# First loads, the first gate and up products, and the output's stores rearranged in a fused SSM-convolution and gated-MLP kernel

## The chip, the cores and the metric

The kernel runs on one core of one Trainium2 chip. A core has a matrix engine (TensorE, PE in the profile), a vector engine (VectorE, DVE), a scalar engine (ScalarE, ACT), GpSimd (POOL) and SyncE (SP), which here only issues DMAs. Each engine takes its instructions in the order in which the program holds them. The metric is the device time of one execution in microseconds (us). Something within about 1% cannot be told from no change with this kernel's three runs.

## The reference

All tensors are bf16, S = 2048 tokens, D = 640 columns, F = 1728. From `x = A_q`, and its layer norm `xn`:

```python
xn  = layernorm(x)
kv  = (sum over t of shift(k, t) * shift_k[:, t]) * v      # 4 taps
y   = causal_conv(kv, ssm_k) + kv * ssm_D                  # long convolution, by FFT in the reference
out = x + xn * y + (sigmoid(xn @ w_gate) * (xn @ w_up)) @ w_down
```

## The kernel before, in words

**Layout.** Token 16p + b lies on partition p in block b, so x is a tile of 128 partitions, 16 blocks and 640 columns. Two strands of work share the engines.

**The MLP strand** goes by four groups t of 512 tokens (four blocks each). Layer norm of a block: statistics on DVE (`ln_stats`), the reciprocal root on POOL (`ln_rstd`), `ln_nmr` on DVE, and `xn` on ACT, DVE or POOL (`ln_xn`). `xn_tr` transposes a block of xn on PE (five 128x128 transposes into PSUM) and ACT or DVE copies it to `xnT`. Then for each of 13 slices fc of 128 columns of F: `gate(fc)` is five matmuls of 512 columns and a sigmoid on ACT; `up(fc)` is five matmuls and a product on DVE into `hT`. `both` does the remaining 64 columns of gate and up at once. `down` is 14 matmuls in two parts of seven for one block and one half of the output's columns, and an addition on DVE into x. These PSUM tiles rotate through the four buffers of pool `psG`.

**The convolution strand** goes by five chunks c of 128 columns. DVE makes kv (`kv_op`, 16 operations per chunk); `h_tr` transposes the filter (16 transposes on PE, two copies on ACT); `add_D` on POOL puts ssm_D into its first tap. The long convolution is a two-stage Fourier transform as matmuls: `st1` (8 per chunk, ACT evicts), `wr1` to DRAM, `rd2` back in another order, `st2` (4 per chunk, ACT evicts), products on DVE (`prod`), `inv1` (2 per chunk, ACT evicts), `wr2` to DRAM, `rdb` back, and `inv2` (2 per chunk, 16 matmuls each), after which DVE multiplies by xn (L409) and adds to x (L410). `rdb` has one buffer `bi`, so the second read of a chunk is issued only when the first `inv2` of that chunk is done. These PSUM tiles rotate through the two buffers of pool `psC`.

**Order.** All of it is written out by a planner at build time. The head (the loads, the layer norm and transposes of group 0, `h_tr(0)`) is written by hand. Then the planner walks PE's time with its own costs (`free`, `ready`, durations in each step), emits the MLP steps `seq` one after another, and puts convolution steps between them when its model says that their inputs are there. `side` issues DMAs, POOL steps and DVE steps; `DUE` says from which MLP step on the next group's layer norm goes ahead of kv on DVE, and `slack` how far ahead of time each kind of load may be issued. The planner runs nothing on the chip: what it fixes is the order of the instructions on each engine and on the DMA queue of SP. At most eight DMAs are outstanding, since the ninth waits for the semaphore of the first.

**The head before** (L413 to L437): ACT's queue issues the filter h of chunk 0 (512 KB); SP's queue issues x block by block (four DMAs of 160 KB), w columns 0 to 255 of gate and up, the taps, k and v of chunk 0, w columns 256 to 767, and the table S1. PE does the four blocks' transposes, then `h_tr(0, 0)` and `h_tr(0, 1)`, then `gate(0)`.

**The end before.** Each of the 16 blocks is stored by one DMA of 160 KB (`store`, L265), which needs the last chunk's `inv2` of its half (blocks 0 to 7 or 8 to 15) and both `down` additions of its block. All 16 stand behind every other DMA on SP's queue.

Of the kernel before, what the change touches and what calls it, by code (L numbers as in the profile page):

```python
# [19 lines left out]
P = 128  # L20
# [37 lines left out]
def kernel(  # L58
# [67 lines left out]
    def load_x(eng, g, n=4):  # L126
        for b in range(4 * g, 4 * g + 4, n):
            eng.dma_start(x[:, b:b + n, :], xr[:, b:b + n, :])
# [79 lines left out]
            eng.tensor_scalar(xn[:, b, :], x[:, b, :], d["rstd"][:, i:i + 1], d["nmr"][:, i:i + 1],  # L208
                              op0=ALU.mult, op1=ALU.add)

    def xn_tr(g, i, eng="act"):

        pt = psG.tile([P, NC, P], BF16, name="pt", tag="g")
        for c in range(NC):
            nc.tensor.transpose(pt[:, c, :], xn[:, 4 * g + i, c * P:(c + 1) * P], ident[:])  # L215
        dst = xnT[:, :, i * P:(i + 1) * P]
        if eng == "act":
            nc.scalar.copy(out=dst, in_=pt[:, :, :])
        else:
            nc.vector.tensor_copy(dst, pt[:, :, :])  # L220


    sig = {}

    def gate(fc):
        pg = psG.tile([P, 512], F32, name="pg", tag="g")
        for c in range(NC):
            nc.tensor.matmul(pg[:, :], lhsT=w[:, c, fc * P:(fc + 1) * P], rhs=xnT[:, c, :],  # L228
                             start=(c == 0), stop=(c == NC - 1))
        sig[fc] = cv.tile([P, 512], BF16, name="sig", bufs=2)  # L230
        nc.scalar.activation(sig[fc][:, :], pg[:, :], ACT.Sigmoid)  # L231

    def up(fc):
        pu = psG.tile([P, 512], F32, name="pu", tag="g")
        for c in range(NC):
            nc.tensor.matmul(pu[:, :], lhsT=w[:, c, UP + fc * P:UP + (fc + 1) * P], rhs=xnT[:, c, :],  # L236
                             start=(c == 0), stop=(c == NC - 1))
        nc.vector.tensor_tensor(hT[:, fc, :], sig[fc][:, :], pu[:, :], ALU.mult)  # L238

    def both():  # L240
# [20 lines left out]
        if part == 1:  # L261
            nc.vector.tensor_tensor(x[:, b, es], pd[:, :], x[:, b, es], ALU.add)  # L262

    def store(b):
        sync.dma_start(outr[:, b, :], x[:, b, :])  # L265


    def add_D(c):
# [141 lines left out]
        nc.vector.tensor_tensor(x[:, bs, cs], x[:, bs, cs], yx[:, :, :], ALU.add)  # L410


    load_h(0, nc.scalar, 0, 0, S)  # L413
    load_x(sync, 0, 1)
    load_w(sync, 0, 256)
    load_taps(0)
    load_halo(0)
    load_k(0, 0, NB)
    load_v(0, 0, NB)
    load_w(sync, 256, 768)  # L420
    sync.dma_start(S1t[:], S1d.ap())

    for i in range(4):
        ln_stats(0, i)
        ln_rstd(0, i, i + 1)
        if i:
            ln_nmr(0, i - 1, i)
            ln_xn(0, i - 1, "act")
        if i == 2:
            xn_tr(0, 0)  # L430
        if i == 3:
            xn_tr(0, 1)
    ln_nmr(0, 3, 4)
    ln_xn(0, 3)
    xn_tr(0, 2)
    xn_tr(0, 3, "dve")
    add_D(0)  # L437
    h_tr(0, 0)
    h_tr(0, 1)

    free = dict(PE=15.5, ACT=15.5, DVE=15.0, POOL=14.0, SP=15.0, DMA=20.0)
    ready = dict(S1=22.0, kx0=15.0, v0=17.0)
    ready.update({("w", f): 14.0 if f < 2 else 18.5 for f in range(6)})
    ready.update({("taps", 0): 15.0,
                  ("h", 0, 0): 16.0, ("h", 0, 1): 17.0})
    count = dict(C=0, G=0)  # L450
    BIG = 1e9

    def when(need):
# [6 lines left out]
    def emit(step):  # L460
        fn, args, ops = step
        ops = ops()
        fn(*args)
        for eng, dur, need, make in ops:
            at = when(need)
            if eng == "DMA":
                free["SP"] = max(free["SP"], at) + 0.45
                free["DMA"] = max(free["DMA"], free["SP"] + 1.4) + dur
                end = free["DMA"] + 0.7
            else:  # L470
                free[eng] = max(free[eng], at) + dur
# [93 lines left out]
    for c in range(NC):  # L565
        if c:
# [8 lines left out]
            for i in range(4):  # L575
# [3 lines left out]
            chains["pool2"] = chains.get("pool2", [])  # L579
            chains["pool2"].append((taps, (c,), lambda c=c: [("POOL", 0.75, [("sraw", c), ("kvn", c - 1, 13)],  # L580
                                                              [("taps", c)])]))
            chains["front"] += [s_htr(c, 0), s_htr(c, 1)]
        chains["kv"] += [s_kv(c, [8 * h + n for n in ns]) for h in range(2)
                         for ns in ((0,), (1, 2), (3, 4), (5, 6), (7,))]
        chains["front"] += [s_st1(c, n) for n in range(8)]
# [18 lines left out]

    bulk = chains["bulk"]
    bulk.append((sync.dma_start, (SMt[:], SMd.ap()), lambda: [("DMA", 0.2, [], ["SM"])]))
    bulk += [s_w(768, 1280), s_x(1), s_w(1280, FF)]
    bulk += chains["sp_k"][:5] + [s_wd(0, 7), s_wd(7, NFC)] + chains["sp_v"][:4] + chains["sp_h"][:2]
    del chains["sp_k"][:5], chains["sp_v"][:4], chains["sp_h"][:2]
    chains["bulk2"] = bulk = [s_x(2), s_x(3)]  # L610
    bulk.append((sync.dma_start, (TBt[:], TBd.ap()), lambda: [("DMA", 2.9, [], ["TB"])]))
# [54 lines left out]
    for b in range(NB):  # L666
        last = [("xa", NC - 1, b // 8), ("dn", b, 1)]
        chains["out"].append(s_load(store, (b,), 0.7, last, []))

    pos = {k: 0 for k in chains}  # L670

# [93 lines left out]
```

## Time and profile before

| what | us |
|---|---|
| median of 3 runs (252.27 to 253.85) | 253.43 |
| the profiled execution | 254.8 |
| its span, from the first to the last recorded event | 252.9 |
| PE busy, 2428 matmuls | 235.4 |
| DVE busy | 179.0 |
| ACT busy | 150.0 |
| POOL busy | 27.8 |
| first matmul starts | 8.28 |
| first `gate` starts | 13.72 |
| last matmul ends | 248.79 |

The span is cut into 40 slices of 6.3 us on the page, and a digit there is a busy share in tenths. The timeline gives an instruction or a run of equal ones by its start and length; a note in brackets says how long its engine had been idle and what ended it. A matmul's recorded length includes its way through the array (379 ns for 512 columns), while the distance between starts of equal matmuls is the pace (216 ns for 512 columns). The profiled execution is 1.4 us above the median of the runs; sums below are made against it and then moved to the median.

### The profile page before, as it was taken

The numbers are of one execution on the slowest core, as the hardware profiler recorded it, in microseconds if no ns is written. First come the engines' busy times: TensorE is split into PE (matmuls) and PEld (weight loads), VectorE is DVE, ScalarE is ACT, GpSimd is POOL, SyncE is SP. The second block draws the span as 40 slices with busy tenths as digits, with TensorE's granted clock in tenths as the row PEclk, the third lists the DMA queues.
The fourth block names the chain that finished last, engine by engine and source line by source line (L and its number), as shares of the span: only waits on it lengthen the run. The fifth ranks groups of instructions, "written<-read, shape, count | busy, mean of one in ns | idle before, by whom it ended". The sixth has DMA issues, their size and how long they took to land.

```text
span 252.9 us, 5862 instructions
## 1 busy us (share of the span) xinstructions
PE 235.4 (93%) x2428; PEld 138.3 (55%) x2428; DVE 179.0 (71%) x312; ACT 150.0 (59%) x186; POOL 27.8 (11%) x40
## 2 busy tenths in 40 slices
PE   0499999889999999999999999999999989999993
PEld 0454455557755554556765545656666435445772
DVE  2749999499889999599999992156718284674361
ACT  2744471428988788873676678966577754463000
POOL 4300118020001070701100000000000000000000
PEclk9999999999999999999999999999999999999999
DMA  6999989999998999879755423697247582303285
GB/s 183 264 326 345 351 183 358 294 259 234 268 264 310 246 307 289 218 209 345 237 184 176 132 95 135 233 281 271 83 161 216 131 238 91 86 3 84 84 287 212
DMA packets 84310, 54.84 MB, mean 217 GB/s; under 512 B 46844, under 2 KB 77372, under 8 KB 84028
## 3 DMA queue, kind: packets, MB, share of 16 engines
q1 hardware_dynamic: 83996, 53.95, 72.8%
q10 hardware_dynamic: 288, 0.52, 0.6%
q8 instruction: 19, 0.31, 0.5%
q14 instruction: 7, 0.06, 0.1%
HBM read 36.12 MB, written 18.35 MB: 215 GB/s over the span
## 4 chain that ended last, share of the span: by engine, by line
PE 69%; DMA 23%; DVE 2%; ACT 2%; SPq 1%; issue 1%; ACTq 0%
PE pg L228 17%; PE pu L236 17%; PE pd L259 17%; DMA bi<-d 9%; DMA d<-t 6%; PE ps L319 5%; PE psb L405 4%; DMA TBt<-tabTB 3%; PE psa L377 3%; PE ps L347 3%; DMA t<-d 2%; DMA x<-in_A_q_dram 2%; PE pht L277 2%; PE pt L215 2%; DMA d<-ao 2%; DVE st L187 1%
## 5 line engine op out<-in xcount | busy, mean ns | idle before, releaser
L259 PE MATMUL pd<-wd,hT 128*128 128x320 bf16 x448 | 65.5, 300 | 0.0
L228 PE MATMUL pg<-xnT,w 128*128 128x512 bf16 x260 | 64.8, 380 | 0.0
L236 PE MATMUL pu<-xnT,w 128*128 128x512 bf16 x260 | 64.7, 380 | 0.0
L238 DVE TENSOR_TENSOR hT<-sig,pu 128x512 bf16<-128x512 bf16 x52 | 35.3, 681 | 35.7 <-PE pu L236 25.8
L259 PEld LDWEIGHTS <-hT 128*128 128x128 bf16 x448 | 42.5, 98 | 17.7 <-issue 1.8
L231 ACT ACTIVATE sig<-pg 128x512 bf16<-128x512 f32 x52 | 31.2, 602 | 31.8 <-PE pg L228 31.4
L350 ACT CAST xz<-ps 128x1024 bf16<-128x1024 f32 x40 | 38.5, 1017 | 12.0 <-PE ps L347 11.7
L322 ACT CAST t<-ps 128x1024 bf16<-128x1024 f32 x40 | 39.1, 1018 | 9.6 <-PE ps L319 5.4
L228 PEld LDWEIGHTS <-w 128*128 128x128 bf16 x260 | 24.8, 98 | 27.2 <-issue 1.3
L236 PEld LDWEIGHTS <-w 128*128 128x128 bf16 x260 | 24.5, 98 | 27.2 <-issue 1.4
L262 DVE TENSOR_TENSOR x<-pd,x 128x320 bf16<-128x320 f32 x32 | 15.5, 488 | 14.8 <-PE pd L259 14.4
L361 DVE TENSOR_TENSOR xz<-xz 128x2048 bf16<-128x2048 bf16 x20 | 24.5, 1224 | 0.6
L382 ACT CAST ao<-psa 128x1024 bf16<-128x1024 f32 x20 | 19.3, 1017 | 8.1 <-PE psa L377 4.5
L298 DVE TENSOR_TENSOR acc<-acc,tmp 128x1024 bf16<-128x1024 bf16 x30 | 21.9, 729 | 1.0
L319 PE MATMUL ps<-kvh,S1t 128*128 128x256 bf16 x160 | 21.9, 273 | 0.0
L296 DVE TENSOR_TENSOR tmp<-kx,sc 128x1024 bf16<-128x1024 bf16 x30 | 20.6, 686 | 0.1
L319 PEld LDWEIGHTS <-S1t 128*128 128x128 bf16 x160 | 15.4, 98 | 5.8 <-issue 0.3
L187 DVE BATCH_NORM_STATS2 st<-x 128x6 f32<-128x320 bf16 x32 | 14.0, 478 | 4.6 <-DMA x<-in_A_q_dram 4.6
L409 DVE TENSOR_TENSOR yx<-psb,xn 128x1024 bf16<-128x1024 f32 x10 | 12.2, 1220 | 6.2 <-PE psb L405 6.1
L215 PE MATMUL pt<-ident,xn 128*128 128x128 bf16 x80 | 7.7, 242 | 9.5 <-ACT xn L204 9.5
L278 ACT COPY kvh<-pht 128x1024 bf16<-128x1024 bf16 x10 | 10.1, 1017 | 8.2 <-PE pht L277 8.1
L359 DVE STREAM_SHUFFLE xz<-xz 128x512 f32<-128x512 f32 x20 | 14.5, 725 | 0.0
(40 smaller groups left out, 149.1 us busy)
## 6 DMA issues: line engine op xcount, KB each, us to landing
d<-t SPq DMA_DIRECT2D x20, 512.0 KB, 4.1
t<-d SPq DMA_DIRECT2D x20, 512.0 KB, 5.7
d<-ao SPq DMA_DIRECT2D x10, 512.0 KB, 4.5
bi<-d SPq DMA_DIRECT2D x10, 512.0 KB, 4.4
out_dram<-x SPq DMA_DIRECT2D x16, 160.0 KB, 2.6
kx<-in_A_k_dram SPq DMA_DIRECT2D x16, 128.0 KB, 3.8
kvh<-in_A_v_dram SPq DMA_DIRECT2D x16, 128.0 KB, 4.4
hn<-in_A_ssm_k_dram SPq DMA_DIRECT2D x8, 256.0 KB, 4.2
```

The costliest lines, as they stand in the source:

```text
L228: nc.tensor.matmul(pg[:, :], lhsT=w[:, c, fc * P:(fc + 1) * P], rhs=xnT[:, c, :], start=(c == 0), stop=(c == NC - 1))
L231: nc.scalar.activation(sig[fc][:, :], pg[:, :], ACT.Sigmoid)
L236: nc.tensor.matmul(pu[:, :], lhsT=w[:, c, UP + fc * P:UP + (fc + 1) * P], rhs=xnT[:, c, :], start=(c == 0), stop=(c == NC - 1))
L238: nc.vector.tensor_tensor(hT[:, fc, :], sig[fc][:, :], pu[:, :], ALU.mult)
L259: nc.tensor.matmul(pd[:, :], lhsT=hT[:, fc, bb * P:(bb + 1) * P], rhs=wd[:, fc, es], start=(fc == 0), stop=(fc == NFC - 1))
L296: nc.vector.tensor_tensor(d["tmp"][:, :, :], kx[:, lo + 3 - m:hi + 3 - m, :], sb(m), ALU.mult)
L298: nc.vector.tensor_tensor(d["acc"][:, :, :], d["acc"][:, :, :], d["tmp"][:, :, :], ALU.add)
L319: nc.tensor.matmul(ps[:, i, :], lhsT=S1[:, b, h, :], rhs=cin[c]["kvh"][:, b, :, :], start=True, stop=True)
L322: nc.scalar.copy(out=d["t1"][:, o:o + 4, :, :].rearrange("p b s c -> p b (s c)"), in_=ps[:, :, :])
L350: nc.scalar.copy(out=d["xz"][:, 0:2, 4 * n:4 * n + 4, :].rearrange("p s k c -> p k s c"), in_=ps[n].rearrange("p q e s c -> p (q e) s c"))
L361: nc.vector.tensor_tensor(xz[:, 1:3, :, :], xz[:, 0:1, :, :].to_broadcast((P, 2, 8, P)), xz[:, 1:3, :, :], ALU.mult)
L382: nc.scalar.copy(out=dst[:, 2 * n:2 * n + 2, :, :], in_=ps[n].rearrange("p g (s f) -> p g s f", s=2))
```

## The change

- The four blocks of x go out alternately from SP's and ACT's queues, as the first DMAs of each; h of chunk 0 follows on ACT's queue. w is loaded in pieces of 256 columns, interleaved with the taps, k and v; S1 moves behind w columns 768 to 1023.
- `gate` and `up` of fc = 0 and 1 are done in halves of 256 tokens (`half`): the first halves, as soon as two blocks are transposed; then the second halves. The transposes of blocks 2 and 3 stand between the first halves and use `psC`. One of the copies moves from ACT to DVE.
- `h_tr(0, *)` leaves the hand-written head and is placed by the planner like the other chunks'; in the new order it stands right behind the halves.
- The planner's starting state, `DUE`, `slack` and the latency it allows a DMA (0.7 to 1.2) are changed, so the order of the whole program changes.
- `store` takes a range of blocks and columns: columns 0 to 511 of blocks 0 to 11 in pairs, as soon as chunk 3 and `down` are done; columns 512 to 639 of blocks 0 to 7 and of 8 to 11 in one DMA each; blocks 12 to 15 whole.

```diff
-    def xn_tr(g, i, eng="act"):
+    def xn_tr(g, i, eng="act", pool=None):
-        pt = psG.tile([P, NC, P], BF16, name="pt", tag="g")
+        if pool is None:
+            pt = psG.tile([P, NC, P], BF16, name="pt", tag="g")
+        else:
+            pt = pool.tile([P, NC, P], BF16, name="pt", tag="c")
...
+    halves = {}
+    def half(u, fc, n):
+        if n == 0:
+            halves[u, fc] = psG.tile([P, 512], F32, name="pg", tag="g")
+        ns = slice(256 * n, 256 * n + 256)
+        o = u * UP + fc * P
+        for c in range(NC):
+            nc.tensor.matmul(halves[u, fc][:, ns], lhsT=w[:, c, o:o + P], rhs=xnT[:, c, ns],
+                             start=(c == 0), stop=(c == NC - 1))
     def gate(fc):
+        if (0, fc) in halves:
+            half(0, fc, 1)
+            pg = halves.pop((0, fc))
+        else:
...
-    def store(b):
-        sync.dma_start(outr[:, b, :], x[:, b, :])
+    def store(b0, b1, lo, hi):
+        sync.dma_start(outr[:, b0:b1, lo:hi], x[:, b0:b1, lo:hi])
...
-    load_h(0, nc.scalar, 0, 0, S)
-    load_x(sync, 0, 1)
+    for i in range(4):
+        (sync, nc.scalar)[i % 2].dma_start(x[:, i, :], xr[:, i, :])
     load_w(sync, 0, 256)
     load_taps(0)
+    load_h(0, nc.scalar, 0, 0, S)
+    load_w(sync, 256, 512)
     load_halo(0)
     load_k(0, 0, NB)
+    load_w(sync, 512, 768)
     load_v(0, 0, NB)
-    load_w(sync, 256, 768)
-    sync.dma_start(S1t[:], S1d.ap())
...
-        if i == 2:
-            xn_tr(0, 0)
-        if i == 3:
-            xn_tr(0, 1)
+        if i > 1:
+            xn_tr(0, i - 2, ("act", "dve")[i - 2])
     ln_nmr(0, 3, 4)
     ln_xn(0, 3)
-    xn_tr(0, 2)
-    xn_tr(0, 3, "dve")
+    for fc in range(2):
+        half(0, fc, 0)
+        if fc == 0:
+            xn_tr(0, 2, pool=psC)
+        else:
+            xn_tr(0, 3, "dve", pool=psC)
+        half(1, fc, 0)
+    for fc in range(2):
+        gate(fc)
+        up(fc)
     add_D(0)
-    h_tr(0, 0)
-    h_tr(0, 1)
...
-                end = free["DMA"] + 0.7
+                end = free["DMA"] + 1.2
...
-            chains["front"] += [s_htr(c, 0), s_htr(c, 1)]
+        chains["front"] += [s_htr(c, 0), s_htr(c, 1)]
...
-    bulk += [s_w(768, 1280), s_x(1), s_w(1280, FF)]
-    bulk += chains["sp_k"][:5] + [s_wd(0, 7), s_wd(7, NFC)] + chains["sp_v"][:4] + chains["sp_h"][:2]
+    bulk.append(s_w(768, 1024))
+    bulk.append((sync.dma_start, (S1t[:], S1d.ap()), lambda: [("DMA", 2.9, [], ["S1"])]))
+    bulk += [s_w(1024, 1280), s_w(1280, FF), s_x(1), s_wd(0, 7), s_wd(7, NFC)]
+    bulk += chains["sp_k"][:5] + chains["sp_v"][:4] + chains["sp_h"][:2]
...
-        for fc in range(13):
+        for fc in range(0 if t else 2, 13):
...
+    for b in range(0, 12, 2):
+        chains["out"].append(s_load(store, (b, b + 2, 0, 4 * P), 1.2,
+                                    [("xa", NC - 2, b // 8), ("dn", b + 1, 1)], []))
+    for b in (0, 8):
+        e = 8 if b == 0 else 12
+        chains["out"].append(s_load(store, (b, e, 4 * P, DM), 0.25 * (e - b),
+                                    [("xa", NC - 1, b // 8), ("dn", e - 1, 1)], []))
+    for b in range(12, NB):
+        chains["out"].append(s_load(store, (b, b + 1, 0, DM), 0.7,
+                                    [("xa", NC - 1, 1), ("dn", b, 1)], []))
...
-    DUE = (14, 50, 58)
-    slack = dict(bulk=3.0, sp_k=1.5, sp_v=1.5, sp_h=1.5, bulk2=1.5)
+    DUE = (8, 48, 68)
+    slack = dict(bulk=3.0, sp_k=3.0, sp_v=3.0, sp_h=2.0, bulk2=2.0)
```

More of the change, by code (lines that the diff above doesn't have):

```diff
@@ L223 @@
     sig = {}
-    def gate(fc):
[L226 to L229, printed above, removed]
+    halves = {}
[7 more added lines that the diff above has]
+                             start=(c == 0), stop=(c == NC - 1))
+    def gate(fc):
+        if (0, fc) in halves:
+            half(0, fc, 1)
+            pg = halves.pop((0, fc))
+        else:
+            pg = psG.tile([P, 512], F32, name="pg", tag="g")
+            for c in range(NC):
+                nc.tensor.matmul(pg[:, :], lhsT=w[:, c, fc * P:(fc + 1) * P], rhs=xnT[:, c, :],
+                                 start=(c == 0), stop=(c == NC - 1))
         sig[fc] = cv.tile([P, 512], BF16, name="sig", bufs=2)
@@ L233, in up @@
     def up(fc):
[L234 to L237, printed above, removed]
+        if (1, fc) in halves:
+            half(1, fc, 1)
+            pu = halves.pop((1, fc))
+        else:
+            pu = psG.tile([P, 512], F32, name="pu", tag="g")
+            for c in range(NC):
+                nc.tensor.matmul(pu[:, :], lhsT=w[:, c, UP + fc * P:UP + (fc + 1) * P], rhs=xnT[:, c, :],
+                                 start=(c == 0), stop=(c == NC - 1))
         nc.vector.tensor_tensor(hT[:, fc, :], sig[fc][:, :], pu[:, :], ALU.mult)
@@ L428 @@
             ln_xn(0, i - 1, "act")
-        if i == 2:
-            xn_tr(0, 0)
-        if i == 3:
-            xn_tr(0, 1)
+        if i > 1:
+            xn_tr(0, i - 2, ("act", "dve")[i - 2])
     ln_nmr(0, 3, 4)
     ln_xn(0, 3)
-    xn_tr(0, 2)
-    xn_tr(0, 3, "dve")
-    add_D(0)
-    h_tr(0, 0)
-    h_tr(0, 1)
[L445 to L450, printed above, removed]
+    for fc in range(2):
+        half(0, fc, 0)
+        if fc == 0:
+            xn_tr(0, 2, pool=psC)
+        else:
+            xn_tr(0, 3, "dve", pool=psC)
[3 more added lines that the diff above has]
+        up(fc)
+    add_D(0)
+    free = dict(PE=14.5, ACT=14.7, DVE=15.2, POOL=11.0, SP=11.0, DMA=17.0)
+    ready = dict(kx0=15.0, v0=19.0)
+    ready.update({("w", f): 14.0 if f < 4 else 17.0 for f in range(6)})
+    ready.update({("taps", 0): 14.0, ("D", 0): 14.0, ("va", 0): 0.0})
+    ready.update({("C", 0): 11.0, ("C", 1): 12.0})
+    ready.update({("G", k): 13.0 + 0.6 * k for k in range(4)})
+    count = dict(C=2, G=4)
     BIG = 1e9
@@ L665 @@
     per = 27 + 16 + 4
-    for b in range(NB):
-        last = [("xa", NC - 1, b // 8), ("dn", b, 1)]
-        chains["out"].append(s_load(store, (b,), 0.7, last, []))
+    for b in range(0, 12, 2):
[8 more added lines that the diff above has]
+                                    [("xa", NC - 1, 1), ("dn", b, 1)], []))
     pos = {k: 0 for k in chains}
```

## The prediction

> **What bounds the kernel now.** I read the slices first, then the chain of work that ended last, the waits of PE, and the timeline at both ends.
>
> ```profile
> PE   0499999889999999999999999999999989999993
> DVE  2749999499889999599999992156718284674361
> DMA  6999989999998999879755423697247582303285
> ...
> PE 69%; DMA 23%; DVE 2%; ACT 2%; SPq 1%; issue 1%; ACTq 0%
> ```
>
> PE is full from slice 3 to slice 37 and carries 69% of the chain; the DMA share is reads and writes between the convolution's stages. DVE is nearly full up to slice 24, the DMA engines up to slice 19. So the time is PE's work, plus PE's late start, plus its waits, plus the tail behind its last product.
>
> To separate these I put PE's instructions in their order and added their paces from the timeline (start to start): 1.08 us for five matmuls of 512 columns, 0.95 for seven of `down`, 0.44 for an `st1`, 0.47 for `st2`, 0.88 for `inv1`, 0.90 for `inv2`, 0.49 for eight transposes of h, 0.28 for five of xn. A start minus the work ahead of it I call the lag. The first `gate` has 2.1 us ahead of it and starts at 13.72: lag 11.6. The last `inv2` has 226.1 ahead and starts at 242.98: lag 16.9. So 5.3 us are lost between them, and 9.9 pass from there to the end of the span (252.9).
>
> ```profile
> PE psb L405 <- DMA bi<-d: 1.9, 4, 1.0
> PE pg L244 <- ACT sig L231: 0.7, 1, 0.7
> PE pht L277 <- DMA hn<-in_A_ssm_k_dram: 0.6, 1, 0.6
> PE psb L405 <- DMA TBt<-tabTB: 0.4, 1, 0.4
> PE ps L347 <- DMA t<-d: 0.3, 1, 0.3
> ```
>
> These waits (total, times, longest) make 3.9 of the 5.3; the other 1.4 is in small pieces. Nearly all are transfers that the order allowed too little time; the 0.7 is ACT standing 3.8 us for a write of `t1` that took 9.37.
>
> **The head.**
>
> ```profile
> 1.21 0.40 ACTq L136 DMA_DIRECT2D hn<-in_A_ssm_k_dram  x1
> ...
> 3.68 0.89 DVE L187 BATCH_NORM_STATS2 st<-x 128x6 f32<-128x320 bf16 x2 [3.68 <-DMA x<-in_A_q_dram]
> 5.89 0.89 DVE L187 BATCH_NORM_STATS2 st<-x 128x6 f32<-128x320 bf16 x2 [0.90 <-DMA x<-in_A_q_dram]
> 7.19 0.88 DVE L187 BATCH_NORM_STATS2 st<-x 128x6 f32<-128x320 bf16 x2
> ...
> 12.02 1.91 PE L277 MATMUL pht<-ident,hn 128*128 128x128 bf16 x16
> ...
> 13.72 1.39 PE L228 MATMUL pg<-xnT,w 128*128 128x512 bf16 x5
> ```
>
> DVE waits 0.90 for the second block of x while h's 512 KB move beside it; after that a block takes 1.30. With h behind x, the second block comes between 3.7 (with the first) and 5.89 (as now); I take 4.2, since the two blocks' 320 KB are what has moved by 4.0 now. Then the second block's statistics start at 4.95 in place of 5.89, and everything behind comes 0.94 earlier: xn of block 1 on ACT at 7.67 to 8.59, its transposes (0.72 alone) to 9.36, its copy on DVE to 9.88. There the first halves start: 9.9. A half is five matmuls of 256 columns; four of them take 0.44 in `st1`, so 0.54, and two halves cost what one group of five costs. w's first columns, landed by 9.5 now, are issued about 1 us earlier.
>
> But PE isn't at pace there:
>
> ```profile
> 58.02 0.66 PE L277 MATMUL pht<-ident,hn 128*128 128x128 bf16 x8
> ```
>
> Sixteen transposes at 12.02 take 1.91, eight at 58.02 take 0.66: less the 0.23 that one needs, 0.112 apart against 0.062. Full pace comes at about 13.9, within the first `gate`, 2.9 after PE's work became dense at 10.98. I take the same 2.9 behind 9.9 and double the paces until 12.8: half 10.98, transposes of block 2 11.54, half 12.62, then half 13.3, transposes 13.6, half 14.1; the last copy is done at 14.25 and releases the second halves, 2.2 us to 16.4, then `h_tr` to 17.4. By then 6.5 us of work are done: **lag 10.9**, a gain of 0.7. If PE were at pace from 9.9, the second halves would run from 12.8 to 15.0, lag 9.6; if it came to pace only after them, lag 12.6.
>
> [...]
>
> **Between head and tail.** I went through each wait in the new order, with lag and work as above.
> - The reads `bi`. From `inv1`'s start to the landing of the first `bi` the last chunk needs 11.1 (2.8 to the end of ACT's copies at 228.90, 3.9 for the write, 4.4 for the read). The work between: chunk 3 had 11.6 (wait 0.98), now 15.3; chunk 4 had 11.9, now 12.5; chunk 2 13.6 both times (0.41, the read was issued late, behind a write that waited for ACT).
> - The second `bi` needs 1.05 for the `inv2` before it and 3.98 to 6.79 to land. Chunk 4 had 4.7 (wait 0.25), now 5.65; chunk 3 6.1, now 7.1; chunk 2 7.6 (0.25), now only 5.6: a wait between 0 and 2.2. The 6.79 had two `rd2` and two writes beside it, the new place has one of each behind it, so I take 0.4.
> - TB (0.4): its load stands behind chunk 3's h, which needs `h_tr(2, 1)`; from there to `inv2` PE has 12.2 us of work, issue and landing take 1.3 and 7.8. Hidden.
> - h of chunk 1 (0.63): its issue stands behind a `t1` write that waits for ACT; ACT 2.2, issues 1.3, landing 4.2, POOL 0.4 make 8.1, PE has 9.9. Hidden.
> - The write of `t1` that held ACT (0.65): between the `st1` that fills it and the one that needs its buffer PE has 7.1; ACT's 2.2 and a landing of 4.1 to 9.4 make 6.3 to 11.6. The k, v and w_down loads that stood beside it are now issued ahead of it, so I take the low end; the high end costs the 0.65 again.
> - Early loads: by the slices' rates 7.1 MB have moved by 25.3 and 9.3 by 31.6. S1 is now behind 6.1 MB, needed at 29.3; w_down behind 9.7, needed at 44. Hidden; where one slips, what it lacks goes straight into PE. SP's issues are all moved with them: 8 outstanding transfers still hold over 2 MB.
> - DVE: kv begins behind the fourth `hT` at 22.5 rather than 16.9, and must give `st1(0, 0)` its first half by 29.3; nine operations of 0.6 to 0.72 make 5.8 and the last takes 0.69: 29.0. Hidden with 0.3.
>
> I keep the 1.4 of small pieces and add 0.4: **1.8 in place of 5.3**. The last `inv2` has 230.0 of work ahead and starts at 230.0 + 10.9 + 1.8 = 242.7.
>
> **The tail.**
>
> ```profile
> 242.98 1.05 PE L405 MATMUL psb<-bi,TBt 128*128 128x128 bf16 x16 [0.25 <-DMA bi<-d]
> 243.87 4.92 PE L259 MATMUL pd<-wd,hT 128*128 128x320 bf16 x35
> ...
> 245.33 0.69 DVE L410 TENSOR_TENSOR x<-x,yx 128x1024 bf16<-128x1024 bf16 x1
> ...
> 249.44 0.40 SPq L265 DMA_DIRECT2D out_dram<-x  x1
> ```
>
> Now 35 products of `down` follow the last `inv2`, and eight stores go out from 246.05, one each 0.48, the last at 249.44; 3.46 later the span ends. In the new order only seven products follow. Behind the `inv2` (1.05) DVE needs 2.02 until a store may go; five remain, the last of which starts 4 x 0.48 later, and 3.46 end the span: 8.5 in place of 9.9. The six early stores stand on SP ahead of chunk 4's `wr2`, but need only sums that are ready 4 us or more before; the store of columns 512 to 639 of blocks 0 to 7 stands behind the last read, as stores did beside it before (3.98).
>
> The first of the five is 128 KB in pieces of 256 bytes. The write `d<-ao` has such pieces: 512 KB issued at 228.93 let the read go at 232.81, so 3.88; at the 340 GB/s of the stores that is 1.5 of transfer and 2.4 of latency, against 2.1 for a store (2.6 less 0.48). So I charge no more for them.
>
> [...]
>
> **Sum.** 242.7 + 8.5 = 251.2 of span, 1.7 less than 252.9. Against its own execution 254.8 - 1.7 = 253.1; the profiled execution stood 1.4 above the median of the runs, so I forecast **251.7**, 0.7% less. In other words: head -0.7, waits -3.5, and +2.5 at the end, because 3.9 us more of PE's work now stand ahead of the last `inv2` and only 1.4 is saved behind it.
>
> **Rivals.**
> - A, the forecast, 0.40; its own terms (second block of x, the 0.4 and the 1.4, the landing of `t1`) give 250.2 to 253.2.
> - B, PE is at pace early, lag 9.6: 250.4. For it: work now begins denser and two transposes earlier. Against: the 2.9 of the row. 0.22.
> - C, PE comes to pace only behind the halves, lag 12.6: 253.4. [...] 0.10.
> - D, the order doesn't do what it is written for: the waits move but stay 5.3: 251.7 + 3.5 = 255.2. For it: the old order was also planned without waits, and lost 3.9 to them. Against: the margins above. 0.14.
> - E, slower: DVE becomes the bound in the second fifth, from the first `down` addition to the product of `both` of group 1. In order, and at paces start to start, DVE has 57.5 us there and PE 56.3. Before, 52.9 us of DVE's work took 59.8 (49.43 to 109.20), 6.9 lost. A product may be 3.2 late before PE needs its PSUM buffer. If DVE loses L, PE waits 1.2 + L - 3.2; with the old 6.9 that is 4.9, and 251.7 + 4.9 = 256.6. It decides from L = 3.7 on. Against it: 4.2 of the 6.9 were waits for PE and ACT (2.34, 1.10, 0.80), which go when DVE is the late one. 0.14.
>
> From these: faster by over 1% (under 250.9, about what this kernel's measurement can tell from no change) B and a third of A, 0.38; within 1% the rest of A, C, most of D, 0.46; slower a third of D and most of E, 0.16. The range reaches from B with A's good ends, 248.2, to D, 255.6.
>
> **What would show it.** In the profile after: the second block's statistics at about 5; first products of 256 columns at about 9.9 and 0.2 apart, at 0.108 only from 12.8; the first 512-column `gate` at 17.4; `inv2` without a DMA in its brackets but for chunk 2; the last `inv2` near 242.7, ending 8.5 before the span does. It is wrong if DVE shows full slices from 7 to 17 with PE waiting on `hT`, or if transfers of k and v hold `t1` and `rd2` around 45 to 60.

## The result, and the profile after

The changed kernel takes **256.59 us** (median of 16 runs, 254.32 to 259.41) against 253.53 (251.95 to 256.78): ratio 1.012, 95% interval 1.008 to 1.015. It is slower by 1.2%, where 0.7% less was forecast. Its profiled execution took 256.47 with a span of 254.7 (before: 254.8 and 252.9).

In the forecast's own terms (lag: start minus TensorE's work ahead of it) the span comes apart like this:

| | before | forecast | after |
|---|---|---|---|
| lag at the first whole `gate` | 11.6 | 10.9 | 10.9 |
| lost from there to the last `inv2` | 5.3 | **1.8** | **5.4** |
| work ahead of the last `inv2` | 226.1 | 230.0 | 230.0 |
| last `inv2` starts | 242.98 | 242.7 | 246.32 |
| from there to the end | 9.9 | 8.5 | 8.4 |
| span | 252.9 | 251.2 | 254.7 |

One term is off, by all of the 3.5 of span. (The whole miss is 4.9, from 251.7 to 256.59; the rest of it is the move to the median.) First the slices and the chain of the changed kernel's page:

```profile
PE   0699999969999999999979999999999999999990
DVE  4526997678999999999998854626674287553252
DMA  6999999789999997962799826548726673823243
...
PE 42%; DVE 5%; DMA 4%; issue 0%; DVEq 0%
```

TensorE is full but for two dents, slices 8 (50.9 to 57.3) and 20, counted from 0; DVE is full from slice 10 to 20, the DMA engines nearly so up to slice 14. The waits of TensorE (total, times, longest) fill the dents:

```profile
PE pht L300 <- POOL hn L293: 2.5, 1, 2.5
PE pht L300 <- DVE yx L432: 1.4, 1, 1.4
PE psb L428 <- DMA bi<-d: 0.8, 2, 0.5
```

Of the waits for `bi`, 1.9 before, 0.8 is left; TB, `t1` and t2 are gone as forecast. In their place stand two new waits at transposes of h, 3.9 together. They come to more than the 3.5 because the small pieces make only 0.7 of the 5.4, where 1.4 was forecast. TensorE's timeline (start, duration, in brackets the wait and who ended it) has the forecast's other points:

```profile
9.90 1.23 PE L237 MATMUL pg<-xnT,w 128*128 128x256 bf16 x5 [0.68 <-ACT xn L204]
...
17.39 0.38 PE L247 MATMUL pg<-xnT,w 128*128 128x512 bf16 x1
...
55.23 1.21 PE L300 MATMUL pht<-ident,hn 128*128 128x128 bf16 x16 [2.50 <-POOL hn L293]
...
129.69 0.66 PE L300 MATMUL pht<-ident,hn 128*128 128x128 bf16 x8 [1.36 <-DVE yx L432]
...
246.32 1.06 PE L428 MATMUL psb<-bi,TBt 128*128 128x128 bf16 x16
```

The halves start at 9.9 and the first whole `gate` at 17.4, as forecast. The lag then holds at 11.0 up to 52.7 and jumps to 13.7, and at 129.7 to 15.4.

**The first jump.** POOL's addition of D waits for h of chunk 1. SP's timeline says when that went out:

```profile
45.08 3.21 SPq L159 DMA_DIRECT2D kvh<-in_A_v_dram  x4
48.39 0.45 SPq L351 DMA_DIRECT2D d<-t  x1
48.88 0.43 SPq L135 DMA_DIRECT2D dcl<-in_A_ssm_D_dram  x1
49.41 1.31 SPq L136 DMA_DIRECT2D hn<-in_A_ssm_k_dram  x2
```

and ACT's when the `t1` ahead of it was ready:

```profile
42.84 1.93 ACT L345 CAST t<-ps 128x1024 bf16<-128x1024 f32 x2 [1.11 <-PE ps L342]
...
52.17 1.93 ACT L345 CAST t<-ps 128x1024 bf16<-128x1024 f32 x2 [4.84 <-DMA d<-t]
```

`t1` was ready at 44.77; its write went out at 48.39, since SP was giving out ten loads of k and v of chunk 1 from 37.1 to 48.3, about 1.1 each. The issues themselves were that long, 0.5 to 1.9, with three to seven of SP's transfers under way; SP's waits between 34 and 52 show only this one ahead of a load of k or v:

```profile
SPq L159 <- DMA wd<-in_B_w_down_dram: 0.2, 1, 0.2
```

It is the limit of eight outstanding transfers, met once (in the trace at most eight are under way at any time): the first load of v could go at 45.08 because the transfer eight places ahead had landed at 45.06. For the other nine that transfer had landed 1.2 to 5.2 earlier. What stretches an issue the trace doesn't show; in the profile before, the same ten lasted 7.6 together, here 10.7. The first half of h landed at 54.4, POOL's addition ended at 55.1, and TensorE had come for it at 52.7. The write, too, was late for someone: ACT stood 4.84 for it.

**The second jump.** The PSUM buffer of the transposes at 129.69 is freed by DVE's `yx` of chunk 0. Its matmuls were done at 126.6; DVE came to it at 128.42. TensorE's and DVE's timelines:

```profile
125.54 1.06 PE L428 MATMUL psb<-bi,TBt 128*128 128x128 bf16 x16
```

```profile
119.24 1.20 DVE L315 TENSOR_TENSOR acc<-kx,sc 128x1024 bf16<-128x1024 bf16 x1
...
121.53 1.59 DVE L384 TENSOR_TENSOR xz<-xz 128x2048 bf16<-128x2048 bf16 x1
...
123.75 1.17 DVE L321 TENSOR_TENSOR acc<-acc,tmp 128x1024 bf16<-128x1024 bf16 x1
...
128.42 1.22 DVE L432 TENSOR_TENSOR yx<-psb,xn 128x1024 bf16<-128x1024 f32 x1
```

Three of these took 1.20, 1.59 and 1.17 where their groups take 0.69, 1.23 and 0.69 elsewhere: 1.35 more, the size of the wait. POOL normalised blocks beside them, also more slowly (5.73 for four, 3.45 elsewhere):

```profile
118.66 5.73 POOL L208 TENSOR_SCALAR xn<-x,rstd,nmr 128x640 bf16<-128x640 bf16 x4
```

### The profile page after: what moved, and what is told of

It reads as the page before. It is cut to its first block, busy times and chain, and to the rows that moved or that the text cites. A ratio compares the mean times of both kernels' runs of the same rounds, so it can differ in the third digit from the quotient of the medians.

```text
span 254.7 us, 5907 instructions
## 1 busy us (share of the span) xinstructions
PE 235.1 (92%) x2448; PEld 139.0 (55%) x2448; DVE 178.9 (70%) x313; ACT 149.5 (59%) x185; POOL 27.3 (11%) x40
## 4 chain that ended last, share of the span: by engine, by line
PE 42%; DVE 5%; DMA 4%; issue 0%; DVEq 0%
PE pd L282 11%; PE pu L259 11%; PE pg L247 10%; DMA bi<-d 4%; PE psb L428 3%; PE ps L342 2%; PE psa L400 2%; PE ps L370 1%; DVE acc L321 1%; DVE yx L432 1%; PE pg L267 1%; DVE tmp L319 1%; PE pht L300 1%; DVE xz L384 1%; DVE x L285 1%; DVE acc L315 0%
## 5 line engine op out<-in xcount | busy, mean ns | idle before, releaser
L282 PE MATMUL pd<-wd,hT 128*128 128x320 bf16 x448 | 66.8, 299 | 0.0
L259 PE MATMUL pu<-xnT,w 128*128 128x512 bf16 x250 | 62.2, 379 | 0.0
L247 PE MATMUL pg<-xnT,w 128*128 128x512 bf16 x250 | 62.2, 379 | 0.0
L261 DVE TENSOR_TENSOR hT<-sig,pu 128x512 bf16<-128x512 bf16 x50 | 34.0, 679 | 32.8 <-PE pu L259 24.5
L247 PEld LDWEIGHTS <-w 128*128 128x128 bf16 x250 | 23.6, 98 | 27.4 <-issue 1.4
L259 PEld LDWEIGHTS <-w 128*128 128x128 bf16 x250 | 23.5, 98 | 27.0 <-issue 1.6
L321 DVE TENSOR_TENSOR acc<-acc,tmp 128x1024 bf16<-128x1024 bf16 x30 | 21.2, 708 | 1.0
L208 POOL TENSOR_SCALAR xn<-x,rstd,nmr 128x640 bf16<-128x640 bf16 x12 | 12.6, 1066 | 1.1 <-DVE nmr L197 0.9
```

What stands on the lines that cost most here:

```text
L282: nc.tensor.matmul(pd[:, :], lhsT=hT[:, fc, bb * P:(bb + 1) * P], rhs=wd[:, fc, es], start=(fc == 0), stop=(fc == NFC - 1))
L321: nc.vector.tensor_tensor(d["acc"][:, :, :], d["acc"][:, :, :], d["tmp"][:, :, :], ALU.add)
```

## The experiments

All ratios are to the kernel before, run beside each on the same chip. "Lost" is the table's second row. The code lines are short forms: they say what changes in the order, not the edit line for line.

### One wait at a time, and a part of the change undone

`after_h1`: in the list of loads, h of chunk 1 goes ahead of v of chunk 1.

```
-    bulk += chains["sp_k"][:5] + chains["sp_v"][:4] + chains["sp_h"][:2]
+    bulk += chains["sp_k"][:5] + chains["sp_h"][:2] + chains["sp_v"][:4]   # the planner's times kept
```

> The changed kernel, with the loads of D and h of chunk 1 moved on SP ahead of the four loads of v of chunk 1 (they were behind them and behind a write of t1); nothing else moves on any engine. In the changed kernel the transposes of that h start at 55.23 after a wait of 2.50, and SP gives h's two loads out only at 49.4 to 50.7, after ten loads of k and v that take it from 37.1 to 48.3. Theory (the 3.5 us missing against the forecast are two waits, this one and 1.36 at the transposes of chunk 3): h's loads go out at about 45 to 46.5, land 4.4 later at 50.9, POOL is done by 51.5, PE comes at 52.7: the wait goes, DVE's idle time of 1.64 and 0.63 behind it goes with it, span 252.3 to 252.5 (2.2 to 2.4 less), time 254.3, ratio to the kernel before 1.003. Rival (DVE, gapless from 63 to 137, is the bound, and PE's waits only show where it is met): PE is early by 2.5 at 53 and gives it back at the transposes of chunk 3, whose wait grows from 1.36 to about 3.5; span at least 254.2, ratio 1.010. Second rival: v, now 1.4 later, is late instead: a wait of 1 to 2 for kvh at the first products of chunk 1.

Measured: 1.013 (1.006 to 1.020), span 254.5. h went out at 45.7, and the transposes waited all the same, for ACT, which waited for the `t1` write that h had overtaken. TensorE's and ACT's timelines:

```profile
54.75 0.66 PE L300 MATMUL pht<-ident,hn 128*128 128x128 bf16 x8 [1.96 <-ACT t L345]
```

```profile
53.69 1.93 ACT L345 CAST t<-ps 128x1024 bf16<-128x1024 f32 x2 [6.29 <-DMA d<-t]
```

Neither theory: a third thing behind the same queue was as late as h. The wait at chunk 3 did not grow (1.16). That says nothing about DVE, because TensorE came to it no earlier (at 128.50, against 128.33 in the changed kernel).

`after_yx`: on DVE, a pair of the convolution of chunk 4 goes behind the read-out (`yx` and the sum) of chunk 0.

```
-    kv_ops(4, [5, 6]); inv2(0, 1)
+    inv2(0, 1); kv_ops(4, [5, 6])
```

> The changed kernel, with one pair of DVE instructions of the convolution of chunk 4 (tmp and acc, 1.4 us) moved behind the two instructions of the read-out of chunk 0, blocks 8 to 15 (yx and the addition to x); loads and PE order are the same. In the changed kernel PE waits 1.36 at 129.69 for that yx, which frees its PSUM buffer; the matmuls it reads are done at 126.6, and DVE comes to it only at 128.42. Theory: yx runs from about 127.0 to 128.2, the wait of 1.36 goes to under 0.2, nothing waits for the pair that went back; span 253.4 (1.2 to 1.4 less), ratio 1.007. Rival (DVE is the bound over the whole stretch): the 1.36 comes back as waits for hT or for the convolution of chunk 3 or 4 between 130 and 160; span 254.5 or more, ratio 1.012.

Measured: 1.003 (1.000 to 1.007), 254.61. `yx` ran at 127.26, the transposes at 128.63 without a wait:

```profile
128.63 0.66 PE L300 MATMUL pht<-ident,hn 128*128 128x128 bf16 x8
```

Nothing came back: lost 4.5, the end at 254.1 though the first whole `gate` was 0.36 later. So the theory holds here, and the 1.4 goes when DVE's order is changed.

`after_h1_yx`: both.

> Both edits: h of chunk 1 ahead of v, and the read-out of chunk 0 ahead of the last pair of the convolution of chunk 4. Theory: both waits go, 2.3 and 1.3 less, span 251.1, which is the span that was forecast for the change itself (251.2); time 252.9, ratio to the kernel before 0.997. Rival (DVE the bound from 63 to 137): the second edit can only give back what the first gained, span about 253.2, ratio 1.006.

Measured: 1.008 (1.004 to 1.012), 255.85, not better than `after_yx` alone, whose interval it overlaps. The profile lost 3.4, with 1.90 waiting for ACT's `t` as in `after_h1`.

`after_whole`: the halves undone.

```
-    for fc in range(2):
-        half(0, fc, 0)
...
-        half(1, fc, 0)
+    xn_tr(0, 2, pool=psC)
+    xn_tr(0, 3, "dve", pool=psC)
```

> The changed kernel without halves: the first two pairs of gate and up run whole, behind all transposes of the first four blocks; everything behind them is in the same order. Theory: the first gate starts at about 13.3 with 1.1 us of work ahead of it, at half pace until 2.9 us later, so that the first gate of the third pair, at 17.39 in the changed kernel, comes 1.3 (PE at pace) to 2.7 (half pace) later; but the transposes of h of chunk 1 wait for a load that SP sets and not PE, so their wait shrinks from 2.50 to between 0 and 1.2, and the span is at most 0.5 longer (254.7 to 255.2), ratio 1.012 to 1.014. Rival (the start of the kernel passes through to its end): the span is 1.3 to 2.7 longer, ratio 1.017 to 1.023.

Measured: 1.028 (1.021 to 1.035), 260.79. The first part came as expected: the third pair's `gate` starts at 18.93 instead of 17.39, the wait for h shrinks to 0.29, and at the first `down` product of the second pass the lag is 13.8 in both. Then `bi` of chunk 0 came 2.34 late, and TensorE's clock fell. The read had gone out at 101.88 instead of 100.13, behind the same issues on SP: D and the first half of h of chunk 3 took 3.09 and 1.61 there, 2.62 and 0.37 in the changed kernel. The profile by stretches (from:to and its length, then PE, PEld, DVE, ACT and POOL, granted clock, DMA share, GB/s):

```profile
110.00:111.00 1.00, 0.05 (x1) 0.09 (x2) 0.00 (x0) 0.00 (x0) 0.00 (x0) 0.99 1.12 336
111.00:112.00 1.00, 1.00 (x11) 1.00 (x12) 0.00 (x0) 0.00 (x0) 0.00 (x0) 0.50 1.15 285
...
113.00:114.00 1.00, 1.00 (x6) 0.52 (x5) 1.00 (x1) 0.00 (x0) 0.00 (x0) 0.50 0.12 27
```

Half pace from 110.98 to 114.39 cost another 1.7 (0.76 and 0.97 more lag). So the kernel is slower without the halves, but not through the head alone: up to 106 their 1.5 was worth nothing. Why those two issues were longer stays open.

### The queue as one cause, and the stores

`after_t1h1`: v of chunk 1 behind both the `t1` write and h.

```
+    bulk: k(1); write of t1(0, 1); D, h(1); v(1)      # was k(1); v(1); t1(0, 1); D, h(1)
```

> The changed kernel with v of chunk 1 moved on SP behind two things that stood behind it: the second write of t1 of chunk 0, and the loads of D and h of chunk 1. Nothing else moves. With h alone moved ahead, the transposes of h waited 1.96 all the same, now for a PSUM buffer: ACT's evictions into t stood 6.29 us until that write of t1 had landed, which SP gave out at 49.5 though t was ready at 44.8. Theory (SP's row of k and v loads is the one cause behind both waits, 2.50 for h and 1.96 for t): the write goes out at 45.1, h at 45.5 to 47, the evictions wait no longer, and the transposes start with no wait over 0.3 (at 52.5 to 53); the first st2, at 65.2 now, comes 1.0 to 2.3 earlier, and the span is 1.0 to 2.3 shorter than 254.7; ratio 1.003 to 1.008. Rival (DVE, gapless from 63, is the bound): the wait goes at 53, but the one at the transposes of chunk 3 grows from 1.2 to 3 or more, and the span stays above 254.2; ratio 1.011. Second rival: v, later by 2.3, is late for the convolution and PE waits 1 or more for kvh near 55.

Measured: 1.010 (1.006 to 1.014), span 254.8. The transposes start at 53.17 with no wait, the first `st2` at 63.84 instead of 65.32: lag 12.3 up to 106. And then:

```profile
108.50 1.05 PE L428 MATMUL psb<-bi,TBt 128*128 128x128 bf16 x16 [1.31 <-DMA bi<-d]
```

The same `inv2` stood at 108.40 in the changed kernel. Its `bi` was read at 99.82 (100.13 there), although the write that it reads went out 1.3 earlier. SP's timeline:

```profile
93.66 0.38 SPq L412 DMA_DIRECT2D d<-ao  x1
94.14 3.65 SPq L135 DMA_DIRECT2D dcl<-in_A_ssm_D_dram  x1
...
99.82 0.57 SPq L419 DMA_DIRECT2D bi<-d  x1
```

The load of D held SP for 3.65 in between, but the read did not wait for it. The write took 6.1 to land (5.1 in the changed kernel), so until 99.75, and the read went out 0.07 later. The wait for h was taken away and a later one gave the time back.

`after_best`: also v of chunk 2 behind two reads of t2, and the read-out moved as in `after_yx`.

> As before (the t1 write and h of chunk 1 ahead of v of chunk 1), and v of chunk 2 behind the first two reads of t2, and the read-out of chunk 0 ahead of the last pair of the convolution of chunk 4. Theory: the waits of 2.5 and 1.4 both go and nothing takes their place: span 251.0 to 251.8, the forecast of the change itself, time 252.8 to 253.5, ratio 0.992 to 0.998. Rival (DVE the bound from 63 to 137): no more than the read-out alone gave, ratio 1.002 to 1.004, with PE's lag at the second pass near that of the changed kernel.

Measured: 1.016 (1.009 to 1.023). v of chunk 2 then stood ahead of chunk 1's `t1` writes; TensorE's waits:

```profile
PE ps L370 <- DMA t<-d: 2.4, 1, 2.4
PE psb L428 <- DMA bi<-d: 0.7, 1, 0.7
```

`after_old_stores` and `before_new_stores`: each kernel with the other's stores.

```
+    for b in range(NB): store(b, b + 1, 0, DM)      # in the changed kernel
+    the six, two and four stores of the change      # in the kernel before
```

> The changed kernel with the sixteen stores of whole blocks that the kernel before has, all behind the last transform write; nothing else moves. Forecast step: the stores in parts shorten the time behind the last inv2, because only six stores are left behind it. Theory: eight stores of 0.48 follow the last sum at about 249.4, the last starts at 252.8, 3.46 later the end: span 256.2 to 256.4, 1.5 to 1.7 longer than 254.7; ratio 1.018. Rival (the end is set by the transfer's landing and not by SP's issues): at most 0.4 longer, ratio 1.013.

> The kernel before with the stores of the changed kernel: six of two blocks by 512 columns, two of the last 128 columns, four whole blocks. Theory: in this order five steps of down follow the last inv2, the last sum of a block ends near 249.1 and its store starts at 249.4 with either set, so the span is at most 0.4 shorter than 252.9; ratio 0.998 to 1.002. Rival (fewer stores behind the last sum are worth 1.4 here too): span 251.5, ratio 0.994 to 0.995.

Measured: 1.021 (1.012 to 1.030) and 0.999 (0.995 to 1.004). In the profiles the span ends 27.93 behind the last `inv1` with sixteen stores and 26.48 with twelve: 1.45, in the order of the change. In the order before, the time is the same. Both as expected. This second profile, 250.4 long, also lost only 3.3 where the first one of that order lost 5.3.

### Four slower kernels and what held them

`after_fix`: `after_t1h1`, `after_yx`, and D and h of chunk 3 behind the first read of `bi`. `after_fix2`: that read instead right behind its write. `fix_warm`: `after_fix` with transposes of the identity on TensorE at the start. `after_gpx`: five large loads on POOL's queue.

```
+    rdb(0, 0); load_h(3, ...)                     # after_fix: was load_h(3, ...), TB, rd2, rdb(0, 0)
+    wr2(1); rdb(0, 0); load_h(3, ...)             # after_fix2
+    nc.gpsimd.dma_start(...)                      # after_gpx: x of blocks 4 to 15, S1, TB
```

> The changed kernel with three moves: the t1 write and h of chunk 1 ahead of v of chunk 1 on SP; D and h of chunk 3 (which SP took 3.5 us to give out, from 95.5 to 99.0) behind the first read of bi of chunk 0; the read-out of chunk 0 ahead of one pair of the convolution of chunk 4 on DVE. v of chunk 2 stays where it was. Theory (waits in a row behind SP's queue: 2.5 for h, then 1.3 for bi of chunk 0, and 1.2 to 1.4 on DVE's order): the read of bi goes out 1.5 us earlier, its wait of 1.31 goes, the lag is 12.3 to 12.7 up to 125 and 14 at the end; span 252.2 to 252.8, ratio 0.998 to 1.003. Rival (a transfer slowed by the others' traffic, not by its place): the wait for bi or t2 comes back at 1 us or more, span 253.5 to 254.5, ratio 1.004 to 1.009.

> The changed kernel with five large loads (x of the blocks 4 to 15 and the two tables S1 and TB, 4 MB) given out by POOL on its own queue instead of SP; the order on SP is otherwise the same. Two theories of why SP stands 8 to 9.5 of every 10 us between 15 and 100. If it is SP's in-order issue (each issue waits until the transfer eight before it has landed, and the large ones hold it longest), SP gets ahead, h of chunk 1 and the t1 write go out 2 or more earlier, the wait of 2.5 falls below 1, and the ratio is 1.003 to 1.008. If it is the transfers themselves (the DMA engines' mean share is 1.0 to 1.1 from 15 to 80), the landing times grow instead, the wait stays at 1.5 or more, and the ratio is 1.010 to 1.015. POOL itself has 89% of its time free.

> The changed kernel with the t1 write and h of chunk 1 ahead of v of chunk 1, the read-out of chunk 0 ahead of one pair of the convolution of chunk 4, and the first read of bi of chunk 0 put on SP right behind the write it reads (ahead of D and h of chunk 3, TB and a read of t2). Theory (three waits in a row, each with its own cause in SP's or DVE's order): bi goes out at about 98 instead of 99.8, its wait of 1.31 falls under 0.4, the read-out does not wait, lag 12.3 to 12.8 up to 125 and 13.7 to 14.3 at the end, span 252.1 to 252.8, ratio 0.998 to 1.004. Rival (DVE, gapless from 47 to 106, is the bound there): PE waits 1 or more for DVE between 100 and 130 instead, span 253.4 or more, ratio 1.005 or more.

> The kernel with the three moves and the same 36 and 8 transposes of the identity at the start. With the clock open at 10 the first halves take 0.55 each instead of 1.0: the second halves start at 12.9 to 13.3 and the first gate of the third pair at 15.2 to 15.8 instead of 17.4 to 17.9. Theory: 1.0 to 2.0 less than the three moves alone as far as transfers allow (w of the columns 512 to 767 must have landed by 18.5), ratio 0.992 to 0.998. Rival (transfers up to 100 set the pace): the same as the three moves alone, within 0.3%.

Measured: `after_fix` 1.015 (1.003 to 1.026), `after_gpx` 1.048 (1.038 to 1.058), `after_fix2` 1.017 (1.011 to 1.022), `fix_warm` 1.018 (1.009 to 1.027). In `after_fix2` the write of `ao` went out at 95.45 and the read behind it could go only at 101.40; D and h of chunk 3 stood behind that. Its POOL, DVE and TensorE timelines, one line each:

```profile
107.72 0.19 POOL L293 TENSOR_TENSOR hn<-hn,dcl 128x1 bf16<-128x1 bf16 x1 [28.28 <-DMA hn<-in_A_ssm_k_dram]
```

```profile
108.91 0.16 DVE L197 SCALAR_TENSOR_TENSOR nmr<-mv,rstd 128x4 f32<-128x4 f32 x1 [2.72 <-POOL rstd L193]
```

```profile
110.90 0.31 PE L282 MATMUL pd<-wd,hT 128*128 128x320 bf16 x1 [2.18 <-DVE hT L271]
```

The late load held POOL, which held DVE behind `rstd` for 2.72, which held TensorE for 2.18: four in-order queues in a row. In `after_fix`, whose profile is of its longest execution, TensorE waited 2.5 for the same `hT` and in `fix_warm` 3.5, where DVE had stood 4.28 for `rstd`. For the read of `bi` these runs speak against the theory of the queue. It went out within 0.1 of its write's landing in `after_fix`, `after_fix2` and `fix_warm`, as it had done in the changed kernel (100.07 and 100.13), so taking D and h out of its way on SP could gain nothing. What the moves cost elsewhere the rows show. `after_gpx`: POOL gave S1 and x out ahead of w, and TensorE's waits were

```profile
PE ps L370 <- DMA t<-d: 6.0, 1, 6.0
PE pg L247 <- DMA w<-in_B_w_gate_dram: 2.7, 2, 1.7
```

SP did not get ahead. Two of its issues became the longest of all, each shortly behind large loads that POOL had given out:

```profile
15.90 9.02 SPq L140 DMA_DIRECT2D sraw<-in_A_shift_k_dram  x1
...
84.42 7.51 SPq L148 DMA_DIRECT2D kx<-in_A_k_dram  x1
```

Behind the first stood w, behind the second the read of t2. The loads of h went out at 52.11, 2.7 later than in the changed kernel; the wait for h shrank to 1.11 only because TensorE itself came 3.55 later. These two rows suggest that an issue on SP is also stretched by what another queue has under way; either way, what went ahead here made others late.

`after_old_due`: the change with the planner's old settings.

```
-    DUE = (8, 48, 68)
+    DUE = (14, 50, 58)      # and slack 1.5, landing 0.7
```

> The changed kernel with the planner's settings of the kernel before (when the statistics of the next blocks are due, how far loads run ahead, and 0.7 instead of 1.2 for a landing); start, loads and stores are those of the change. In its order the last inv1 has 213.9 us of TensorE's work ahead of it (211.8 in the changed kernel, 209.5 in the kernel before), and in all traces so far the span ends 26.4 to 26.5 behind that inv1's start with these stores. Theory (what stands ahead of the last inv1 and the lag make the end): with the lag of 16.4 of the changed kernel the span is 256.8, ratio 1.020. Rival (the settings cause the waits): lag 13 to 14, span 253.3 to 254.3, ratio 1.004 to 1.008.

Measured: 1.034 (1.027 to 1.040): the settings are not what made the change slow; without them it is worse still, by more than the later `inv1` explains. Its profile, of its longest execution (267.57; the others 261.66 to 264.28), has waits of 5.0 for TB and 3.4 for h.

### Fewer transfers

`less_h`: no loads of h and D for chunks 1 to 4, and also the moves of `after_t1h1` and `after_yx`. It leaves out a part of the work.

```
     def load_h(c, eng, n, lo, hi):
+        if c: cin[c]["hn"] = cin[0]["hn"]; return
```

> The changed kernel without the loads of h and D of chunks 1 to 4 (their transposes read h of chunk 0 once more, D is added only there), so 2.1 MB less are loaded, 1.5 MB of them before 105, and no addition of D holds POOL; also the t1 write ahead of v of chunk 1 and the read-out of chunk 0 ahead of one pair of the convolution of chunk 4. Theory (the transfers of the first 105 us are the bound there, and moving one ahead makes another late): with 5 to 6 us of DMA time taken out no wait of over 0.5 is left up to 130, lag 11.2 to 12.5 at the first inv2 of chunk 0, 13.0 to 13.8 at the end, span 251.2 to 252.3, ratio 0.992 to 0.999. Rival (DVE is the bound from 47 to 107): TensorE comes early and waits 1.5 to 2.5 for DVE between 63 and 110, span 253.3 or more, ratio 1.003 or more.

Measured: **0.997 (0.995 to 0.999)**, 253.16, span 251.5, lost 1.95. Apart from the start these are all waits of TensorE on another engine or a transfer:

```profile
PE psb L433 <- DMA bi<-d: 0.7, 1, 0.7
...
PE ps L347 <- DVE kvh L329: 0.4, 1, 0.4
```

DVE had no gap over 0.15 from 47.85 until its 0.80 of idle time at 106, and TensorE waited for it only those 0.4. So at this lag DVE does not give the waits back, and the forecast's 1.8 and 251.2 are nearly met (1.95, 251.5). 2.1 MB of transfers, twelve issues on SP and POOL's additions of D were taken out together, and no run has the two moves without anything else, so this run alone doesn't say which of them it is. For one wait, the one for `bi` of chunk 0, SP's timeline does, beside that of `after_t1h1`:

```profile
93.62 0.38 SPq L417 DMA_DIRECT2D d<-ao  x1
...
98.41 0.54 SPq L424 DMA_DIRECT2D bi<-d  x1
```

The write went out at the same time (93.62, there 93.66) and landed 4.8 later instead of 6.1; the read went out 0.02 behind that and landed 6.5 later instead of 8.5. Neither SP nor POOL held it: the transfers themselves were faster with fewer beside them.

### The kernel before against itself, and TensorE's clock at the start

`before_again` is the kernel before. `before_warm`, `before_warm_b` (the same) and `before_warm2` add transposes of the identity ahead of the first work, and eight more between the first blocks'.

```
+    for i in range(36): nc.tensor.transpose(pw[:, i % 8, :], ident[:], ident[:])     # 60 in before_warm2
```

> The kernel before, unchanged. In the execution behind the forecast its waits between the first gate and the last inv2 came to 5.3; in the run with other stores, whose order is the same up to there, to 3.3. Theory: an execution of this kernel loses 3.3 to 5.3 there by the luck of its transfers, and the one that was profiled lies high; ratio 1.000, within 0.4% either way, and a span of 250.5 to 252.5. Rival: 5.3 is typical, span 252.5 to 253.5.

> The kernel before with 36 transposes of the identity on TensorE from about 1.7 us on and four more behind each of the first two blocks' transposes, into a PSUM buffer that nobody reads; the same results. In its profile the granted clock opens at 14.01, so that three groups of transposes, 16 transposes of h (1.91) and the first 0.3 us of gate run at half pace. Theory (the first 14 us of TensorE are slow because it idles before them, and its lag of 11.6 holds 1.3 of that): the clock opens between 5 and 9, transposes of h take 1.0, the first gate starts at 12.4 to 12.8, span 0.4 to 1.3 shorter (0.7 of it may be given back at the t1 write and the h load, which were waited for 0.65 and 0.63 before), ratio 0.995 to 0.998. Rival: the first gate is early and all of it is given back by 60, ratio 1.000.

> The kernel before with 36 and 8 transposes of the identity at the start, as it ran before at 0.993 with a clock that opened at 13.83, hardly earlier than without them. Theory (chance: that profile had a lag of 11.8 at the start like the kernel before, and fewer waits behind it, by the luck of its transfers): ratio 0.997 to 1.002. Rival (there is a gain that the clock does not explain): ratio 0.991 to 0.996 once more.

> The kernel before with 60 transposes of the identity from 1.7 us on (0.107 each at half pace, to 8.1) and four behind each of the first two blocks' transposes. With 36 of them TensorE was idle from 5.7 to 8.5, the clock opened at 13.83 as without them, and the time was 0.993 of the kernel before all the same. [...]

Measured: 1.000 (0.997 to 1.003) for the kernel before, with 3.9 lost and a span of 252.2; 0.993 (0.990 to 0.996), then 0.997 (0.994 to 1.000), and 1.000 (0.996 to 1.004) with sixty. The clock did not do what was wanted in any of them: it opened at 13.83; at 5.46, closed at 8.88 and opened at 15.70; at 4.50, closed at 11.33 and opened at 14.74. In the last, TensorE's timeline shows a full pace for xn and a half pace again for h:

```profile
1.70 4.84 PE L427 MATMUL pw<-ident 128*128 128x128 bf16 x60 [1.70 <-POOL ident masks.py:199]
8.12 0.45 PE L215 MATMUL pt<-ident,xn 128*128 128x128 bf16 x5 [1.58 <-ACT xn L204]
...
11.70 1.91 PE L277 MATMUL pht<-ident,hn 128*128 128x128 bf16 x16
```

Whether the 0.993 was more than chance stays open: it did not come a second time, and its clock opened as late as without the added work. No other kernel with the whole computation came out faster than the kernel before.

## Why the prediction was wrong

- **Head: right.** Second statistics at 4.83 (4.95 forecast), halves at 9.90, first whole `gate` at 17.39, lag 10.9. That the clock opened 2.8 behind dense work, at 12.7 where 12.8 was forecast, was luck: with nearly the same starts up to 11 it opened between 12.7 and 14.8 in the runs of this start, which makes lags of 10.9 to 11.7. And the head's gain did not last beyond 55, as `after_whole` shows from the other side.
- **h of chunk 1, "8.1, PE has 9.9, hidden": the step that failed, 2.5 of the 3.5.** The chain's terms were ACT 2.2, issues 1.3, landing 4.2, POOL 0.4. The issue was held not by ACT, as the step has it, but by ten loads on SP ahead of it, until 48.4 and not 44.8. SP's own queue was looked at only for when loads land, not for how long it is taken by issuing them; the profile before had a price for it, 7.6 for the same ten. The step on the `t1` write fails by the same 3.6: it allows 2.2 for ACT and the landing, and no time on SP. Its wait was hidden behind h's and came out as 1.96 in `after_h1`. The prediction's last sentence names just this as what would make it wrong; it was given no price.
- **The PSUM buffer behind `yx`: no step at all, 1.36.** DVE's place was costed for `kv` and for rival E, not for the read-out that frees a buffer of psC, and not for three operations that ran longer beside POOL. `after_yx` (1.003, against 1.012) shows that this is worth its 0.8% or so.
- **Reads of `bi`: right in kind.** Chunks 3 and 4 no longer wait, chunk 2 waits 0.27 (0.4 forecast); chunk 1's second read, not listed, waits 0.53.
- **Taking one wait for itself.** The working treats margins as if they were independent. `after_h1`, `after_t1h1` and `after_best` took the wait for h away, and it came back as ACT's `t`, `bi` or t2; of the runs that did so only `less_h`, with fewer transfers, kept the time. What bounds the first 105 us as a whole is argued from that one run, not shown.
- **Tail and end: right**, 8.4 and +2.4 net. The store in pieces of 256 bytes landed 2.0 behind its issue, the four of whole blocks 1.9 to 2.1, so no charge for small pieces shows. In all runs with the twelve stores the end comes 25.6 to 26.5 behind the start of the last `inv1`, whatever stands between; so its place in TensorE's order, 2.3 later than before, is a price that the change pays in every case.
- **The move to the median: wrong.** It took 1.4 off the sum, as if the execution after would also lie 1.4 above its median. It lies 0.1 below. The profiled execution of the kernel before lay high, 5.3 lost, where two more executions of that order lost 3.3 and 3.9. So the change had less to win than the table shows.
- **Rivals.** D was right: the waits moved and stayed at 5.4 (it gave a span of 254.7, as measured, and 255.2 only for the shift). That the size fits is luck, since the 5.3 that it carries over lay high. E gave 256.6, the measured time, for another reason: TensorE waited nowhere for `hT`, DVE took 60.3 for its 57.5 (47.13 to 107.47) and so lost 2.8, not the 3.7 from which E decides; 2.3 of them lie in two gaps behind TensorE's own wait. B and C did not happen.
- **Side sums.** B and a third of A make 0.35 and not 0.38, and B with A's good end 248.9 and not 248.2. The last chunk's read of `bi` landed in 4.0 (232.81 to 236.81) and not 4.4, so it needed 10.7 and not 11.1. None of them bears on the miss.

## What to carry to other kernels

Cost an in-order issuing queue as an engine: write down when each issue can go and how long it may last (0.3 to 9.0 us on SP here), before calling a load hidden. Before moving an issue, look at whether the one behind it waits for the queue or for an earlier transfer to land. Where the DMA engines are as full as they were here (a mean share of 1.01 from 15 to 80), expect a load moved ahead to be another one moved back: with h ahead in `after_h1` the `t1` write held ACT for 6.29 and TensorE for 1.96, and with the wait of 2.50 gone in `after_t1h1` one of 1.31 for `bi` came. So a wait that is removed must be followed to what stands behind it on every queue that it passes. Take the base of a forecast from several executions: one profile of the order before lost 5.3 in its waits, two more 3.3 and 3.9.

## What the runs showed of the hardware that was not expected

- **The clock fell to half in mid-run.** In `after_whole` the granted clock stood at 0.50 from 110.98 to 114.39, behind the wait of 2.34. Sixteen matmuls of `inv2` took 1.86 there and fourteen of `down` 2.94, where they take 1.06 and 2.08 at full pace, and with that the wait cost 4.1. TensorE's timelines show such stretches in the middle of four more runs: `after_fix` (five matmuls of 512 columns took 2.34 at 92.85, elsewhere 1.24), `after_gpx` (2.34 at 99.70), `after_old_due` (seven of `down` took 2.07 at 56.84, elsewhere 1.11) and `after_fix2` (sixteen of `inv2` took 1.39 at 111.41). The changed kernel's wait of 2.50 was longer than that, but its granted clock stayed at 1.00 from 50 to 60, and it cost no more than itself. So the length of the wait alone does not decide it; what does stays open.
- **DVE and POOL ran longer beside each other.** In the changed kernel 0.69 became 1.17 to 1.20 for DVE operations that read two bf16 tensors beside POOL's normalisation, whose mean rose from 0.86 (106.07 to 109.52, where DVE ran no such operation) to 1.43; an addition that reads PSUM (0.48) and a shuffle (0.72) in the same stretch kept their times, and so did one product (0.68). Why, no run here shows.
